# Attention and a mixture of four experts: the first layer of the last three experts as seven block products instead of eight

## The chip, the core and the metric

One core of one Trainium2 chip runs the whole program. Five engines work beside each other: TensorE (PE, matmuls; its weight loads stand as PEld), VectorE (DVE), ScalarE (ACT), GpSimd (POOL) and SyncE (SP), which issues all transfers here. Each runs its own instructions in order and waits for the others by semaphores. The metric is the device time in microseconds (us).

## The reference

```python
def _attn_ref(q, k, v):                       # (2, 8, 576, 64)
    ...
    out_up = np.repeat(out_d, factor, axis=2) # attention over means of 4 rows
    ...
    return (out_up + out_local)               # plus attention within |i - j| < 4

def _moe_ref(x, domain_probs, w1, w2):        # N=1152, D=512, E=4, F=1024
    p = domain_probs / (domain_probs.sum(-1, keepdims=True) + 1e-09)
    for e in range(E):
        h = np.maximum(x @ w1[e], 0.0)
        out += p[:, e:e + 1] * (h @ w2[e])
```

x is the attention's output, 1152 tokens of 512 values. All is float32.

## The kernel before

Steps have names and an engine each. A table, ORDER, puts them in one list, and each engine gets its steps in that order. Attention fills the first 160 us, four half batches a0 to a3, with the matmuls of expert 0 mixed in. Then PE has the experts alone.

An operand of a matmul is split into a high part, rounded to the format that PE takes in one pass, and a low part, the difference. A product is then three: low weight by high x, high by high, high by low. x lies transposed as `xhi` and `xlo`, 4 slices of 128 model values by 1152 tokens. Weights come by 1 MB (`raw`), ACT casts the high part (`whi`, L174), DVE subtracts for the low part (`wlo`, L278), POOL does it for expert 0.

An expert e is done in chunks c of tokens (m00, m01, m02 of 256, m03 of 384; then three of 384 for each of experts 1 to 3). In a chunk, the first layer makes eight tiles of h, f = 0 to 7, each 12 matmuls into one PSUM bank (4 slices of the model by 3 products, `m1`, L734). ACT takes the relu as the high part (`relu`, L741), DVE the low part (`rest`, L745), for the tile of 128 hidden values and all the chunk's tokens. The second layer takes these as weights: 24 matmuls of 512 columns for each 128 tokens (`m2`, L761), and DVE adds the bank, times the token's share, to `acc` (`gather`, L772). The last expert stores its rows. The very last 128 tokens go in two halves of columns.

```python
terms = [(w, x, d) for w, x in ((lo, xhi), (hi, xhi), (hi, xlo)) for d in range(HP)]
for i, (w, x, d) in enumerate(terms):
    nc.tensor.matmul(
        ps[:, :n], w[:, d, cc:cc + P], x[:, d, n0:n0 + n],
```

Buffers of 8 KB a partition are shared, ten in a ring (`s8`): natural rows of q, k and v at first (`k00n`, `v11n`, ...), raw, high and low weights later. PSUM has eight banks: three for the experts (`ps_m`), three for transposes and the like (`ps_g`), two for scores (`ps_s`). SP's loads in the attention are rows of k and q into a part of `acc` (`k11r`, L233), values around a tile of queries (`vw`, L254) and the natural rows (L222).

## Time and profile before

| | |
|---|---|
| runs, us | 495.96, 497.70, 497.76 (median 497.7) |
| span of the profiled execution | 497.3 us, 0.4 below the median |
| PE busy, share of the span | 482.4 us, 97% |
| DVE, ACT, POOL busy | 214.8, 123.5, 54.8 us |
| attention with m00 to m02 | until 160.8 us |
| m03, then experts 1, 2, 3 | from 160.8 us to the end |

The span goes from the first to the last instruction of one profiled execution on the chip. A matmul's record is longer than the distance to the next one, since they are pipelined; what one costs is the length of a run of them divided by their count.

### The profile page before, as it was taken

The page shows a single profiled execution, that of the slowest core. Times are in us where ns is not written, and L with a number is a line of the kernel's source. Part 1 is how long each engine was busy: PE and PEld are TensorE (multiplying, and loading weights), DVE is VectorE, ACT ScalarE, POOL GpSimd, SP SyncE. Part 2 cuts the span into 40 slices and gives each one's busy share as a digit, 9 for nine tenths or more (in the row PEclk, how much of TensorE's full clock was granted, in tenths as well). Part 3 has the DMA queues.
Part 4 walks back from the last instruction along what each step waited for, and adds up shares of the span by engine and source line. Part 5 has one row for each costly group of instructions (what it writes and reads, how often), then busy time and mean ns, then how long its engine had stood idle before and what let it go on. Part 6 is the DMA issues. An engine that isn't in the chain of part 4 may idle for free.

```text
span 497.3 us, 8306 instructions
## 1 busy us (share of the span) xinstructions
PE 482.4 (97%) x3566; PEld 433.8 (87%) x3566; DVE 214.8 (43%) x449; ACT 123.5 (25%) x265; POOL 54.8 (11%) x68
## 2 busy tenths in 40 slices
PE   5999799999999999999999999999999999999997
PEld 5778597888898988989989889899898898998986
DVE  7578858687776252611212516112125261121211
ACT  4555442432231230501101405011014050110110
POOL 4735640140012000000000000000000000000000
PEclk8555989999999999999999999999999999999999
DMA  7893332510600022400000223100002300101001
GB/s 186 206 247 111 77 75 65 123 23 23 213 1 3 0 91 79 153 17 1 0 1 0 77 93 132 38 1 0 1 0 65 105 3 21 43 0 42 22 11 53
DMA packets 39973, 29.88 MB, mean 60 GB/s; under 512 B 26432, under 2 KB 30720, under 8 KB 39936
## 3 DMA queue, kind: packets, MB, share of 16 engines
q1 hardware_dynamic: 39936, 29.35, 20.9%
q8 instruction: 28, 0.46, 0.4%
q14 instruction: 9, 0.07, 0.1%
HBM read 26.99 MB, written 2.36 MB: 59 GB/s over the span
## 4 chain that ended last, share of the span: by engine, by line
PE 91%; DVE 5%; ACT 1%; DMA 1%; issue 1%; SPq 0%; ACTq 0%
PE m03h L734 3%; PE m32h L734 3%; PE m31h L734 3%; PE m30h L734 3%; PE m22h L734 3%; PE m21h L734 3%; PE m20h L734 3%; PE m12h L734 3%; PE m11h L734 3%; PE m10h L734 3%; PE m32o L761 3%; PE m31o L761 3%; PE m30o L761 3%; PE m22o L761 3%; PE m21o L761 3%; PE m20o L761 3%
## 5 line engine op out<-in xcount | busy, mean ns | idle before, releaser
L278 DVE TENSOR_TENSOR wlo<-raw,whi 128x1024 fp32r<-128x1024 f32 x25 | 30.0, 1223 | 5.7 <-ACT whi L174 5.7
L174 ACT CAST whi<-raw 128x1024 fp32r<-128x1024 f32 x32 | 32.3, 1042 | 0.0
L278 POOL TENSOR_TENSOR wlo<-raw,whi 128x1024 fp32r<-128x1024 f32 x7 | 16.7, 2398 | 5.2 <-ACT whi L174 5.1
L761 PE MATMUL m32o<-whi,m32t 128*128 128x512 f32 (+1 forms) x64 | 15.8, 336 | 0.0
L761 PE MATMUL m03o<-whi,m03t 128*128 128x512 f32 x48 | 14.9, 389 | 0.0
L761 PE MATMUL m10o<-whi,m10t 128*128 128x512 f32 x48 | 14.9, 389 | 0.0
L761 PE MATMUL m11o<-whi,m11t 128*128 128x512 f32 x48 | 14.9, 389 | 0.0
L761 PE MATMUL m12o<-whi,m12t 128*128 128x512 f32 x48 | 14.9, 389 | 0.0
L761 PE MATMUL m20o<-whi,m20t 128*128 128x512 f32 x48 | 14.9, 389 | 0.0
L761 PE MATMUL m21o<-whi,m21t 128*128 128x512 f32 x48 | 14.9, 389 | 0.0
L761 PE MATMUL m22o<-whi,m22t 128*128 128x512 f32 x48 | 14.9, 389 | 0.0
L761 PE MATMUL m30o<-whi,m30t 128*128 128x512 f32 x48 | 14.9, 389 | 0.0
L761 PE MATMUL m31o<-whi,m31t 128*128 128x512 f32 x48 | 14.9, 389 | 0.0
L761 PEld LDWEIGHTS m32o<-whi,m32t 128*128 128x128 f32 x64 | 11.1, 190 | 1.2
L761 PE MATMUL m01o<-whi,m01t 128*128 128x512 f32 x32 | 11.5, 412 | 0.0
L761 PE MATMUL m00o<-whi,m00t 128*128 128x512 f32 x32 | 11.2, 407 | 0.0
L741 ACT ACTIVATE m11t<-m11h 128x384 fp32r<-128x384 f32 x8 | 3.9, 492 | 29.3 <-PE m11h L734 29.3
L741 ACT ACTIVATE m12t<-m12h 128x384 fp32r<-128x384 f32 x8 | 3.9, 492 | 29.3 <-PE m12h L734 29.3
L741 ACT ACTIVATE m21t<-m21h 128x384 fp32r<-128x384 f32 x8 | 3.9, 492 | 29.3 <-PE m21h L734 29.3
L741 ACT ACTIVATE m22t<-m22h 128x384 fp32r<-128x384 f32 x8 | 3.9, 492 | 29.3 <-PE m22h L734 29.3
L741 ACT ACTIVATE m31t<-m31h 128x384 fp32r<-128x384 f32 x8 | 3.9, 492 | 29.3 <-PE m31h L734 29.3
L741 ACT ACTIVATE m32t<-m32h 128x384 fp32r<-128x384 f32 x8 | 3.9, 492 | 29.3 <-PE m32h L734 29.3
(388 smaller groups left out, 1217.4 us busy)
## 6 DMA issues: line engine op xcount, KB each, us to landing
raw<-in_moe_w_dram SPq DMA_DIRECT2D x16, 1024.0 KB
vw<-in_v_dram SPq DMA_DIRECT2D x44, 64.0 KB
out_dram<-acc SPq DMA_DIRECT2D x8, 256.0 KB
acc<-in_q_dram SPq DMA_DIRECT2D x12, 144.0 KB
acc<-in_k_dram SPq DMA_DIRECT2D x8, 144.0 KB
q0n<-in_q_dram SPq DMA_DIRECT2D x2, 288.0 KB
k00n<-in_k_dram SPq DMA_DIRECT2D x2, 288.0 KB
k01n<-in_k_dram SPq DMA_DIRECT2D x2, 288.0 KB
```

The lines of the kernel that those rows point to most:

```text
L174: nc.scalar.copy(out_, in_)
L278: engine(f"wlo{nm}.{i}").tensor_tensor(dst, T["raw" + nm][:, sl], T["whi" + nm][:, sl], ALU.subtract)
L734: nc.tensor.matmul(ps[:, :n], w[:, d, cc:cc + P], x[:, d, n0:n0 + n], start=i == 0, stop=i == len(terms) - 1,)
L741: nc.scalar.activation(ht[:, 0, :n], T[f"{nm}h{f}"][:, :n], AF.Relu)
L761: nc.tensor.matmul(ps[:, cs], T[f"{nm}t{f}"][:, hpart, cc:cc + P], w[:, f % 4, cs], start=f == 0 and x == 0, stop=f == KF - 1 and x == 2,)
```

## The change

Experts 1 to 3 get a new first layer. The weights are cut in 2 x 2 (hidden halves by model halves), x as well (model halves by token halves of 576). The eight products of blocks become seven of sums of blocks, with sums shared between them (the form of Strassen's scheme by Winograd). With x's block 11 negated once, most sums of results are additions.

- Sums of x (`sums_of_tokens`): x1, x2, x4 into new tiles `xc`, x3 over block 12, each 576 tokens by 2 slices, in 2 or 3 steps on DVE, split into high and low again by ACT and DVE. Block 11 is negated in place (`xn`). All this stands in ORDER between the matmuls of m03.
- Weights: each expert's first layer in four parts i of 128 + 128 hidden values. A part is loaded into one raw tile r of 7 x 256 (`wl`, 512 KB in two transfers, runs of 512 bytes), three additions on DVE fill places 4 to 6 and rewrite 2 (`ws`), ACT casts the high half (`wh`), DVE makes the low half (`wo`), 1792 elements each. r has one buffer.
- Products (`product`): 12 matmuls of 288 columns, into tiles of two banks, X, Z and Y per part, four such buffers, all of PSUM. Products 1, 6, 7, 4 go one after the other onto X, 5 and 3 onto Z, 2 into Y. Between them results leave X: ACT copies minus X after product 1 and product 6 and minus Z after 5 (`t11`, `t12`, `t22`) and X after 4 (`h21`) into H, and DVE adds Y, Z and X there (`h11`, `h12`, `h22`).
- h stays in float32 (H, all 1152 tokens); relu, high part (`hh`, ACT) and low part (`ho`, DVE) are made per 128 tokens just before the second layer, which runs over nine tiles of tokens and has the matmuls of before (`second`, `g`).
- Second-layer weights come in quarters of 512 KB (`vl`, `vh`, `vo`).
- The ten s8 buffers become five on either side (`s8`, `s8b`); attention's and expert 0's pools end when they are done, and the new tiles take their place. Comments are removed.

A part of the new order, then the core of the code:

```diff
+    p210 t2210 t1210 p710 h1110 vh12 p111 h2210 vo12 p511 t1111 p410 vl11 t2211 p611 h2110 p310 t1211 p211 wo12 p711
...
-    s8 = ctx.enter_context(tc.tile_pool(name="s8", bufs=10))
-    hp_ = ctx.enter_context(tc.tile_pool(name="h", bufs=KF))
-    a1 = ctx.enter_context(tc.tile_pool(name="a1", bufs=1))
-    a2 = ctx.enter_context(tc.tile_pool(name="a2", bufs=2))
-    a3 = ctx.enter_context(tc.tile_pool(name="a3", bufs=3))
-    ps_m = ctx.enter_context(tc.tile_pool(name="ps_m", bufs=3, space=PSUM))
-    ps_s = ctx.enter_context(tc.tile_pool(name="ps_s", bufs=1, space=PSUM))
-    ps_g = ctx.enter_context(tc.tile_pool(name="ps_g", bufs=3, space=PSUM))
+    s8 = ctx.enter_context(tc.tile_pool(name="s8", bufs=5))
+    attn, first, late = ExitStack(), ExitStack(), ctx
+    hp_ = first.enter_context(tc.tile_pool(name="h", bufs=KF, side="right"))
+    s8b = first.enter_context(tc.tile_pool(name="s8b", bufs=5, side="right"))
+    a1 = attn.enter_context(tc.tile_pool(name="a1", bufs=1))
+    a2 = attn.enter_context(tc.tile_pool(name="a2", bufs=2))
+    a3 = attn.enter_context(tc.tile_pool(name="a3", bufs=3))
+    ps_s = first.enter_context(tc.tile_pool(name="ps_s", bufs=1, space=PSUM))
+    ps_g = first.enter_context(tc.tile_pool(name="ps_g", bufs=3, space=PSUM))
+    ps_m = first.enter_context(tc.tile_pool(name="ps_m", bufs=3, space=PSUM))
...
+    def end_attention():
+        attn.close()
+        pool = late.enter_context(tc.tile_pool(name="xc", bufs=1, reuse_waits="tile"))
+        for m in (1, 2, 4):
+            T[f"xc{m}"] = pool.tile([P, 2, 2, NH], F32R, name=f"xc{m}")
+        T["w7"] = late.enter_context(tc.tile_pool(name="w7", bufs=1, reuse_waits="tile"))
+        T["xsums"] = token_sums.enter_context(tc.tile_pool(name="xs", bufs=1, reuse_waits="tile"))
+    def end_sums():
+        token_sums.close()
+        T["qpool"] = late.enter_context(tc.tile_pool(name="q", bufs=2, reuse_waits="tile"))
+    def end_first():
+        first.close()
+        pool = late.enter_context(tc.tile_pool(name="H", bufs=1, side="right", reuse_waits="tile"))
+        T["H"] = pool.tile([P, KF // 2, 2, N], F32, name="H")
+        T["hpool"] = late.enter_context(tc.tile_pool(name="hs", bufs=2, side="right", reuse_waits="tile"))
+        T["w8"] = late.enter_context(tc.tile_pool(name="w8", bufs=2, side="right", reuse_waits="tile"))
+        T["ps"] = late.enter_context(tc.tile_pool(name="ps", bufs=4, space=PSUM, reuse_waits="tile"))
...
+        def add(m, s, x, op, y, deps):
+            def emit():
+                if f"xs{m}" not in T:
+                    T[f"xs{m}"] = T["xsums"].tile([P, 2, NH], F32, tag=f"xs{m}", name=f"xs{m}")
+                at = lambda z: T[f"xs{m}"] if z is None else f32(z)
+                engine(s).tensor_tensor(T[f"xs{m}"], at(x), at(y), op)
+            step(s, "V", deps, emit)
...
+        def split(m, s, deps, out_):
+            step(f"{s}.h", "A", deps, lambda: copy(f"{s}.h", out_()[0], T[f"xs{m}"]))
+            step(f"{s}.l", "V", [f"{s}.h"], lambda: engine(f"{s}.l").tensor_tensor(
+                out_()[1], T[f"xs{m}"], f32(out_()[0]), ALU.subtract))
...
+        own = lambda m: lambda: (T[f"xc{m}"][:, 0], T[f"xc{m}"][:, 1])
+        sub, plus = ALU.subtract, ALU.add
+        read = [f"m03.m{f}" for f in range(KF)]
+        add(1, "x1.s0", B11[1], sub, B12[1], last + ["endattn"])
+        add(1, "x1.s1", None, plus, B11[0], ["x1.s0"])
+        add(1, "x1.s2", None, sub, B12[0], ["x1.s1"])
+        split(1, "x1", ["x1.s2"], own(1))
+        add(1, "x2.s0", None, plus, B22[1], ["x1.l"])
+        add(1, "x2.s1", None, plus, B22[0], ["x2.s0"])
+        split(1, "x2", ["x2.s1"], own(2))
+        add(1, "x4.s0", B21[1], sub, None, ["x2.l"])
+        add(1, "x4.s1", None, plus, B21[0], ["x4.s0"])
+        split(1, "x4", ["x4.s1"], own(4))
+        add(3, "x3.s0", B12[1], sub, B22[1], last + ["endattn"])
+        add(3, "x3.s1", None, plus, B12[0], ["x3.s0"])
+        add(3, "x3.s2", None, sub, B22[0], ["x3.s1"])
+        split(3, "x3", ["x3.s2", "x1.s2"] + read, lambda: B12)
+        for i, s in enumerate(("xn.h", "xn.l")):
+            step(s, "A", ["x1.s2", "m02.m7"] + ([] if i == 0 else []),
+                 lambda i=i: nc.scalar.mul(B11[i], f32(B11[i]), -1.0))
...
+        def load1(i):
+            r = T[f"r{e}{i}"] = T["w7"].tile([P, 7, 256], F32, tag="w7", name=f"r{e}{i}")
+            src = w1[e].rearrange("(c p) (r i f) -> i r p c f", p=P, i=4, f=P)
+            for h in range(2):
+                nc.sync.dma_start(r[:, 2 * h:2 * h + 2].rearrange("p k (d f) -> p (k d) f", d=2), src[i, h])
+        def sums1(i):
+            r, g = T[f"r{e}{i}"], engine(f"ws{e}{i}")
+            g.tensor_tensor(r[:, 4:6], r[:, 0:4:3], r[:, 2:3].to_broadcast([P, 2, 256]), ALU.add)
+            g.tensor_tensor(r[:, 2], r[:, 5], r[:, 0], ALU.add)
+            g.tensor_tensor(r[:, 6], r[:, 1], r[:, 2], ALU.add)
+        def high1(i):
+            w = T[f"wh{e}{i}"] = s8.tile([P, 7, 256], F32R, tag="s8", name=f"wh{e}{i}")
+            copy(f"wh{e}{i}", w, T[f"r{e}{i}"])
+        def low1(i):
+            w = T[f"wo{e}{i}"] = s8.tile([P, 7, 256], F32R, tag="s8", name=f"wo{e}{i}")
+            engine(f"wo{e}{i}").tensor_tensor(w, T[f"r{e}{i}"], f32(T[f"wh{e}{i}"]), ALU.subtract)
+        for i in range(4):
+            step(f"wl{e}{i}", "S", ["endattn"], lambda i=i: load1(i))
+            step(f"ws{e}{i}", "V", [f"wl{e}{i}"], lambda i=i: sums1(i))
+            step(f"wh{e}{i}", "A", [f"ws{e}{i}"], lambda i=i: high1(i))
+            step(f"wo{e}{i}", "V", [f"wh{e}{i}"], lambda i=i: low1(i))
...
+        def high2(q):
+            pool, tag = (s8, "s8") if q < 2 else (T["w8"], "w8")
+            w = T[f"v{e}{q}"] = pool.tile([P, 2, 1024], F32R, tag=tag, bufs=5 if q < 2 else 2, name=f"v{e}{q}")
+            copy(f"vh{e}{q}", w[:, 0], T[f"q{e}{q}"])
+        def low2(q):
+            w = T[f"v{e}{q}"]
+            engine(f"vo{e}{q}").tensor_tensor(w[:, 1], T[f"q{e}{q}"], f32(w[:, 0]), ALU.subtract)
...
+        tokens = {"1": lambda: B11, "5": lambda: (T["xc1"][:, 0], T["xc1"][:, 1]),
+                  "6": lambda: (T["xc2"][:, 0], T["xc2"][:, 1]), "2": lambda: B21, "7": lambda: B12,
+                  "4": lambda: (T["xc4"][:, 0], T["xc4"][:, 1]), "3": lambda: B22}
+        PRODUCTS = {"1": (0, "X", True, "xn.l"), "5": (5, "Z", True, "x1.l"), "6": (2, "X", False, "x2.l"),
+                    "2": (1, "Y", True, "a3.xl2"), "7": (4, "X", False, "x3.l"), "4": (3, "X", False, "x4.l"),
+                    "3": (6, "Z", False, "a3.xl2")}
+        def product(m, i):
+            k, acc_, first_, _ = PRODUCTS[m]
+            if first_:
+                T[f"{acc_}{e}{i}"] = T["ps"].tile([P, 2, 512], F32, tag="ps", name=f"{acc_}{e}{i}")
+            ps = T[f"{acc_}{e}{i}"]
+            hi, lo = tokens[m]()
+            wh, wo = T[f"wh{e}{i}"][:, k], T[f"wo{e}{i}"][:, k]
+            terms = [(w, x, d) for w, x in ((wo, hi), (wh, hi), (wh, lo)) for d in range(2)]
+            for n in range(2):
+                for u, (w, x, d) in enumerate(terms):
+                    nc.tensor.matmul(
+                        ps[:, n, :NH // 2], w[:, d * P:(d + 1) * P], x[:, d, n * (NH // 2):(n + 1) * (NH // 2)],
+                        start=u == 0 and first_, stop=u == 5, skip_group_check=True,
+                    )
+        def into(i, c):
+            at = lambda n: T[f"{n}{e}{i}"][:, :, :NH // 2]
+            dst = H()[:, i, int(c[1]) - 1, (int(c[2]) - 1) * NH:int(c[2]) * NH].rearrange("p (n t) -> p n t", n=2)
+            if c[0] == "t":
+                nc.scalar.mul(dst, at("Z" if c == "t22" else "X"), -1.0)
+            elif c == "h21":
+                nc.scalar.copy(dst, at("X"))
+            else:
+                nc.vector.tensor_tensor(dst, dst, at({"h11": "Y", "h12": "Z", "h22": "X"}[c]), ALU.add)
+        old = [] if e == 1 else [f"ho{e - 1}{t}" for t in range(1, NTOK)] + [f"ho{e - 1}0.{u}" for u in range(2)]
+        wait = {"6": ["t11"], "7": ["t12"], "4": ["h22"], "3": ["t22"]}
+        for i in range(4):
+            for m, (_, _, _, x) in PRODUCTS.items():
+                deps = [f"wo{e}{i}", x, "endfirst"] + [f"{c}{e}{i}" for c in wait.get(m, [])]
+                step(f"p{m}{e}{i}", "P", deps, lambda m=m, i=i: product(m, i))
+            for c, eng, m in (("t11", "A", ["1"]), ("t22", "A", ["5"]), ("t12", "A", ["6"]), ("h22", "V", ["7"]), ("h21", "A", ["4"]),
+                              ("h11", "V", ["2"]), ("h12", "V", ["3"])):
+                more = old if c[0] == "t" or c == "h21" else [f"t{c[1:]}{e}{i}"]
+                step(f"{c}{e}{i}", eng, [f"p{x}{e}{i}" for x in m] + more, lambda i=i, c=c: into(i, c))
...
+        def hrows(t, u):
+            x = H()[:, :, :, t * P:(t + 1) * P]
+            x = x.rearrange("p i r t -> p (i r) t")
+            return x if u is None else x[:, 4 * u:4 * u + 4]
+        def htile(n, t, u):
+            if f"{n}{e}{t}" not in T:
+                T[f"{n}{e}{t}"] = T["hpool"].tile([P, KF, P], F32R, tag=n, name=f"{n}{e}{t}")
+            x = T[f"{n}{e}{t}"]
+            return x if u is None else x[:, 4 * u:4 * u + 4]
+        def hhigh(t, u):
+            nc.scalar.activation(htile("hh", t, u), hrows(t, u), AF.Relu)
+        def hlow(t, u):
+            nc.vector.scalar_tensor_tensor(
+                htile("ho", t, u), hrows(t, u), 0.0, f32(htile("hh", t, u)), ALU.max, ALU.subtract
+            )
+        def final(t):
+            return e == E - 1 and t == NTOK - 1
+        def second(t, v, q):
+            cs = slice(0, DM) if v is None else slice(v * 256, v * 256 + 256)
+            o = f"o{e}{t}{v}"
+            if q == 0:
+                T[o] = T["ps"].tile([P, 512], F32, tag="ps", name=o)
+            for f in (2 * q, 2 * q + 1):
+                for x, (hpart, w) in enumerate((("ho", 0), ("hh", 1), ("hh", 0))):
+                    nc.tensor.matmul(
+                        T[o][:, cs], T[f"{hpart}{e}{t}"][:, f % 4 * 2 + f // 4],
+                        T[f"v{e}{q}"][:, w, f % 2 * 512 + cs.start:f % 2 * 512 + cs.stop],
+                        start=f == 0 and x == 0, stop=f == KF - 1 and x == 2,
+                    )
```

On PE, the first layer of expert 2 begins before like this (m20, first tile of h):

```order
L734 MATMUL m20h0_3107<-xhi_84,wlo120_3032 128x384 [waits DVE_49]
L734 MATMUL m20h0_3107<-xhi_84,wlo120_3032 128x384 x3
L734 MATMUL m20h0_3107<-xhi_84,whi120_3030 128x384 [waits Activation_49]
L734 MATMUL m20h0_3107<-xhi_84,whi120_3030 128x384
L734 MATMUL m20h0_3107<-xhi_84,whi120_3030 128x384 [waits Activation_49]
L734 MATMUL m20h0_3107<-xhi_84,whi120_3030 128x384
L734 MATMUL m20h0_3107<-xlo_85,whi120_3030 128x384 x4
```

and now like this (part 0: products 1, 5 and the begin of 6):

```order
L936 MATMUL X20_3240<-xhi_87,wo20_2974 128x288 x2
L936 MATMUL X20_3240<-xhi_87,wh20_2920 128x288 x2
L936 MATMUL X20_3240<-xlo_88,wh20_2920 128x288 x2
L936 MATMUL X20_3240<-xhi_87,wo20_2974 128x288 x2
L936 MATMUL X20_3240<-xhi_87,wh20_2920 128x288 x2
L936 MATMUL X20_3240<-xlo_88,wh20_2920 128x288 x2
L936 MATMUL Z20_3256<-xc1_2242,wo20_2974 128x288 x2
L936 MATMUL Z20_3256<-xc1_2242,wh20_2920 128x288 x4
L936 MATMUL Z20_3256<-xc1_2242,wo20_2974 128x288 x2
L936 MATMUL Z20_3256<-xc1_2242,wh20_2920 128x288 x4
L936 MATMUL X20_3240<-xc2_2243,wo20_2974 128x288 [waits Activation_49]
```

Twelve matmuls of 384 into one bank have become twelve of 288 into two; Z20 stands between X20 and its next use, which waits for ACT.

On DVE, in the same first layer, before:

```order
L745 SCALAR_TENSOR_TENSOR m20t1_3153<-m20h1_3124,m20t1_3153 128x384 [waits Activation_49]
L278 TENSOR_TENSOR wlo220_3158<-raw220_3120,whi220_3156 128x1024 [waits DMAHW5_49,Activation_49]
L745 SCALAR_TENSOR_TENSOR m20t2_3173<-m20h2_3140,m20t2_3173 128x384 [waits Activation_49]
L278 TENSOR_TENSOR wlo220_3158<-raw220_3120,whi220_3156 128x1024 [waits Activation_49]
L745 SCALAR_TENSOR_TENSOR m20t3_3191<-m20h3_3160,m20t3_3191 128x384 [waits Activation_49]
L278 TENSOR_TENSOR wlo221_3196<-raw221_3122,whi221_3194 128x1024 [waits DMAHW6_49,Activation_49]
```

and now (sums of part 2's weights, h of part 0, the low half wo22):

```order
L878 TENSOR_TENSOR r22_3231<-r22_3231 128x512 [waits DMAHW2_49,DMAHW1_49,DVE_49]
L879 TENSOR_TENSOR r22_3231<-r22_3231 128x256 [waits DVE_49]
L880 TENSOR_TENSOR r22_3231<-r22_3231 128x256 [waits DVE_49]
L949 TENSOR_TENSOR H_2504<-H_2504,Y20_3286 128x576 [waits PE_49,Activation_49]
L949 TENSOR_TENSOR H_2504<-H_2504,X20_3240 128x576 [waits PE_49,Activation_49]
L888 TENSOR_TENSOR wo22_3395<-r22_3231,wh22_3300 128x1792 [waits PE_49,Activation_49]
L949 TENSOR_TENSOR H_2504<-H_2504,Z20_3256 128x576 [waits PE_49]
```

The low half of a weight now stands among additions to H, and it waits for PE, which has still to finish with the buffer it goes to.

On SP, in the attention of the first batch, before (vw05's and vw04's loads, v10n and k11r follow):

```order
L222 DMA v11n_949<-in_v_dram 72x4x256 [waits DMAHW1_49,DVE_49,Pool_49]
L254 DMA vw05_951<-in_v_dram 32x8x64 [waits DMAHW2_49]
L254 DMA vw05_951<-in_v_dram 32x8x64 [waits DMAHW3_49]
L254 DMA vw05_951<-in_v_dram 32x8x64 [waits DMAHW4_49]
L254 DMA vw05_951<-in_v_dram 28x8x64 [waits DMAHW5_49,Pool_49]
```

and now:

```order
L218 DMA v11n_952<-in_v_dram 72x4x256 [waits DMAHW1_49,Activation_49,Pool_49]
L250 DMA vw05_954<-in_v_dram 32x8x64 [waits DMAHW2_49]
L250 DMA vw05_954<-in_v_dram 32x8x64 [waits DMAHW3_49]
L250 DMA vw05_954<-in_v_dram 32x8x64 [waits DMAHW4_49]
L250 DMA vw05_954<-in_v_dram 28x8x64 [waits DMAHW5_49]
```

The load v11n waits for other work of POOL than before; POOL's wlo201, for which v10n waited before, is now what v11n waits for, and v10n no longer waits for it.

## Rows read from the trace of the kernel before

**Rows 1.** the page's busy shares, us, share of the span, instructions
```profile
PE 482.4 (97%) x3566; PEld 433.8 (87%) x3566; DVE 214.8 (43%) x449; ACT 123.5 (25%) x265; POOL 54.8 (11%) x68
```

**Rows 2.** the page's chain that ended last, shares by engine
```profile
PE 91%; DVE 5%; ACT 1%; DMA 1%; issue 1%; SPq 0%; ACTq 0%
```

**Rows 3.** the chain in order of time: start us, us, what
```profile
160.91 16.96 PE m03h L734 x96
177.88 16.32 PE m03o L761 x72
194.19 16.96 PE m10h L734 x96
211.16 16.32 PE m10o L761 x72
...
477.39 16.64 PE m32o L761 x96
```

**Rows 4.** stretches by engine: m03, first layer of expert 1, all of expert 1
```profile
core 0: us, PE busy (x) PEld busy (x) DVE busy (x) ACT busy (x) POOL busy (x), PEclk, DMA share, GB/s
160.75:194.03 33.28, 33.28 (x169) 30.47 (x168) 10.64 (x15) 7.61 (x12) 0.44 (x1) 1.00 0.19 64
194.03:210.99 16.96, 16.96 (x97) 16.95 (x96) 10.05 (x13) 7.18 (x11) 0.00 (x0) 1.00 0.32 103
194.03:293.86 99.83, 99.83 (x505) 91.42 (x504) 30.17 (x42) 19.33 (x32) 0.00 (x0) 1.00 0.14 43
```

**Rows 5.** the same chain, matmuls of 256 columns at the full clock
```profile
102.74 4.25 PE m01h L734 x36
137.41 4.29 PE m02h L734 x36
```

**Rows 6.** groups by line, DVE: busy us, mean ns of one
```profile
L278 DVE TENSOR_TENSOR wlo<-raw,whi 128x1024 fp32r<-128x1024 f32 x25 | 30.0, 1223 | 5.7 <-ACT whi L174 5.7
L745 DVE SCALAR_TENSOR_TENSOR m10t<-m10h,m10t 128x384 fp32r<-128x384 f32 x8 | 4.5, 557 | 5.9 <-ACT m10t L741 5.9
L772 DVE SCALAR_TENSOR_TENSOR acc<-m10o,pr,acc 128x512 f32<-128x512 f32 x3 | 2.3, 751 | 13.7 <-PE m10o L761 13.7
```

**Rows 7.** groups by line, ACT; then a handover in the timeline
```profile
L174 ACT CAST whi<-raw 128x1024 fp32r<-128x1024 f32 x32 | 32.3, 1042 | 0.0
L741 ACT ACTIVATE m10t<-m10h 128x384 fp32r<-128x384 f32 x8 | 3.9, 492 | 21.8 <-PE m10h L734 21.8
...
262.91 0.49 ACT L741 ACTIVATE m12t<-m12h 128x384 fp32r<-128x384 f32 x1 [17.95 <-PE m12h L734]
263.44 0.56 DVE L745 SCALAR_TENSOR_TENSOR m12t<-m12h,m12t 128x384 fp32r<-128x384 f32 x1 [1.89 <-ACT m12t L741]
```

**Rows 8.** stretches of time, the load of 1 MB issued at 181.82 us
```profile
181.80:182.80 1.00, 1.00 (x6) 0.84 (x5) 1.00 (x1) 0.44 (x1) 0.00 (x0) 1.00 0.00 0
182.80:186.80 4.00, 4.00 (x20) 3.30 (x19) 1.26 (x2) 0.00 (x0) 0.00 (x0) 1.00 0.94 305
```

**Rows 9.** timelines of SP, POOL and PE in the attention; chain's longest load
```profile
55.70 0.30 SPq L222 DMA_DIRECT2D v11n<-in_v_dram  x1
56.05 10.72 SPq L254 DMA_DIRECT2D vw<-in_v_dram  x8
67.43 0.94 SPq L233 DMA_DIRECT2D acc<-in_k_dram  x2
...
64.59 2.46 POOL L278 TENSOR_TENSOR wlo<-raw,whi 128x1024 fp32r<-128x1024 f32 x1
...
76.55 0.42 PE L313 MATMUL k11t<-ident,acc 72*128 72x72 f32 x4
...
1.22 4.90 DMA q0n<-in_q_dram
```

**Rows 10.** groups by line, weight loads of PE: busy us, mean ns
```profile
L734 PEld LDWEIGHTS m10h<-xhi,whi 128*128 128x128 f32 x32 | 5.7, 188 | 0.0
L734 PEld LDWEIGHTS m02h<-xhi,whi 128*128 128x128 f32 x32 | 4.3, 188 | 0.0
```

More of the change, by code (lines that the diff above doesn't have):

```diff
@@ L262, in load @@
         def load():
-            t = T["raw" + nm] = s8.tile([P, 4, 512], F32, tag="s8", name="raw" + nm)
+            t = T["raw" + nm] = (s8, s8b)[which - 1].tile([P, 4, 512], F32, tag="s8", name="raw" + nm)
             if which == 1:
@@ new lines, in sums_of_tokens @@
+    def sums_of_tokens():
+        last = [f"a3.xl{t}" for t in range(NT)]
+        step("endattn", "X", last + ["m02.m7"], end_attention)
+        step("endsums", "X", ["x4.l", "x3.l"], end_sums)
+        step("endfirst", "X", ["m03.g2", "endattn"], end_first)
+        def add(m, s, x, op, y, deps):
[29 more added lines that the diff above has]
+                 lambda i=i: nc.scalar.mul(B11[i], f32(B11[i]), -1.0))
@@ L819 @@
             attention(b, half)
-    for e in range(E):
-        for which in (1, 2):
-            for half in range(2):
-                weight(e, which, half)
-        chunks = ((0, 256), (256, 256), (512, 256), (768, 384)) if e == 0 else ((0, 384), (384, 384), (768, 384))
-        for c, (n0, n) in enumerate(chunks):
-            expert(e, c, n0, n)
+    for which in (1, 2):
+        for half in range(2):
+            weight(0, which, half)
+    for c, (n0, n) in enumerate(((0, 256), (256, 256), (512, 256), (768, 384))):
+        expert(0, c, n0, n)
+    sums_of_tokens()
+    for e in range(1, E):
+        late_expert(e)
     plan(steps)
```

245 lines of the change are left out of this document (129 added, 116 removed).

## The prediction

> **What bounds the kernel now.** I read the busy shares first: TensorE (PE) is busy for 482.4 of 497.3 us [rows 1]. A busy PE need not be on the path, so the chain of waits comes next: PE holds 91% of it [rows 2]. Then the chain in order of time: from 160.9 us on it is PE alone, 96 matmuls of a first layer in 16.96 us, 72 of a second in 16.32, in turn, to the last 16.64 us [rows 3]. The stretches by engine agree: one late expert takes 99.83 us, all of it PE at granted clock 1.00, the higher level (2.4 GHz), with VectorE (DVE) at 30.2 and ScalarE (ACT) at 19.3 us beside it [rows 4]. So a late expert costs its matmuls, 3 x 16.96 + 3 x 16.32 = 99.84 us, and what shortens them counts in full as long as the work beside them keeps up.
>
> **First layer: fewer columns, more matmuls.** Before, an expert has 288 matmuls of 384 columns: 50.88 us, 176.7 ns each [rows 3]. After, it has 4 blocks x 7 products x 12 = 336 of 288 columns. No row has 288. At the full clock 36 matmuls of 256 columns took 4.29 us, 119.2 each (another 36: 118.1) [rows 5]; 512 columns take 16.32 / 72 = 226.7 [rows 3]. A straight line from 256 to 384 gives 119.2 + 32/128 x 57.5 = 133.6 ns. Low end: 384 scaled by columns, 132.5. High end: the line through 512 and 384 carried down, 176.7 - 96 x 0.39 = 139.2. I take 133.6, since 256 is the nearest row. 336 x 133.6 = 44.9 us, 6.0 less per expert, **18.0 us less** for three; the ends give 19.1 and 12.3.
>
> **Second layer.** Still 9 x 24 matmuls of 512 columns an expert, the very last tile in halves as before: no change on PE. Beside each tile of 5.44 us ACT has one pass of 1024 elements (1.04), DVE a difference of 1024 (1.22) and the sum into acc (0.75) [rows 6, 7]: hidden.
>
> **What must hide beside a block.** A block is 84 x 133.6 = 11.2 us of PE. From 384 to 1024 elements DVE rows rise by 1.04 ns an element, ACT rows by 0.86 [rows 6, 7]. DVE per block: weight sums of 512, 256 and 256, 1.5; the low half of 1792, 2.0; three additions of 576 out of PSUM at 0.76 to 0.82 (the higher from the row of 751 ns for 512), 2.5; one low half of second-layer weights, 1.2. Sum 7.2 of 11.2. ACT: the high half of 1792, 1.7; four copies of 576 at 0.66; one cast, 1.0: 5.4 of 11.2. The totals fit; three places are narrow.
>
> (a) PE may not add to X again before ACT has copied it. The product on another buffer between them is 12 x 133.6 = 1.6 us, against 0.66 for the copy and 0.04 for a handover (ACT from 262.91 for 0.49, DVE from 263.44 [rows 7]). Hidden, unless ACT is in the middle of a 1.7 us high half.
>
> (b) The low half of block i goes into a buffer that block i-2 read as weights, and the last product of i-2 stands fifth of seven within block i-1. Two products, 3.2 us, are left for a step of 2.0, two handovers and, if DVE is in one, an addition of 0.8: 0.3 us spare.
>
> (c) One raw buffer: a load waits for the low half before it. 1 MB came in 1.0 us of silence and 4.0 at 305 GB/s [rows 8], so half of that needs 3.0 us in runs of the same length; runs of 512 B are not in the trace, and I bound them by 5.0. Load, sums, high, low: 3.0 + 1.5 + 1.7 + 2.0 = 8.2, at most 10.2, of 11.2.
>
> Together these cost 0 at the low end; at the high end each of 12 blocks meets half a DVE addition, 12 x 0.4 = 4.8. I take **1.0 us**, nearer to 0 since each sum fits. If the cover goes, each us of lateness per block costs 12.
>
> **Token sums under the last chunk of expert 0.** On DVE 14 steps of 1152 elements (1.36 each, 19.0), two weight sums and two low halves (7.1) come in, four low halves (4.6) go. DVE was busy 10.6 of 33.3 us there [rows 4]; now some 32. That is nearly full, but the last sum and the last acc of the chunk are first needed four products (6.4 us) into expert 1. Cost 0 to 3, taken 0.5.
>
> **Attention.** One wait moves. SP's queue is in order; the load v11n was issued at 55.70 and now waits for POOL's last low half, which starts at 64.59 and takes 2.46, so until 67.1 [rows 9]. Behind it stand eight vw, v10n and two k11r loads. Before, the first of the last two was issued at 67.43; now 11 issues stand ahead or between at about 0.45 each (two take 0.94), so the second leaves near 72.0 and lands, by the longest load of the chain, 4.90 us [rows 9], at 76.9. PE uses it at 76.55: 0 to 0.4 us late, taken 0. Otherwise the order before m03 is the same but for two swapped low halves on POOL.
>
> **Sum.** 497.3 - 18.0 + 1.0 + 0.5 = 480.8 us of span. The median of the runs, 497.7, lies 0.4 above the profiled span: **481.2 us**. Own range: 497.7 - 19.1 = 478.6 to 497.7 - 12.3 = 485.4, plus up to 4.8 + 3 of waits.
>
> **Rivals.** *A, the weight chain is late:* if 512-byte runs move at half the rate (5.0 us) and two of the steps of (c) find their engine in another step (0.8 on DVE, 0.7 on ACT), the chain is 10.2 + 1.5 + four handovers = 11.9, 0.7 late in the 9 blocks whose load isn't hidden under a second layer: +6.3, 487.5. For it: (c) has least room at its long end; against: 305 GB/s with nothing else on the queues [rows 8].
>
> *B, DVE and ACT run in turn instead of side by side:* both queues are in order, every low half waits for a high half and every addition for a copy. Wholly in turn a block takes 7.2 + 5.4 + a dozen handovers of 0.04 = 13.1 us, 1.9 late, 12 x 1.9 = 23: 504, slower. It decides against the change from 11.2 + 18/12 = 12.7 us a block. Against it: the second layer between experts lets both engines catch up, and most steps do not depend on each other.
>
> *C, a matmul's cost doesn't fall with its columns:* in the first layer the weight loads fill their row, 16.95 of 16.96 us [rows 4], and 336 loads stand where 288 were. At 176.7 ns each that is 59.4 us an expert, 8.5 more, +25.5: 523. It decides from 50.88 / 336 = 151.4 ns a matmul. Against it: loads read 188 ns [rows 10] for 256 columns as well, and those pairs came every 119 ns [rows 5], so loads overlap.
> The Trainium skill, Perfetto Trace Analysis, Identifying the Most-Contended Engine, says to judge TensorE's headroom by the busy share of LDWEIGHTS instead of matmul; by that the first layer has none, and this change adds loads. The same skill, TensorE: Matmul & The Clock Gate, Back-to-back issue gap, gives 81 ns at 128 columns and 131 at 512 for streams of load and matmul; an estimate on its line is 114 at 384 and 102 at 288, hence 336 x 102 - 288 x 114 = +1.4 us an expert, 502. Here 512 columns take 226.7 ns [rows 3], so the trace does not bear that line out.
>
> *D, the products are not fewer than I count:* the order has the 84 matmuls of 288 a block, so only the attention's 0.4 us is left of it.
>
> **Chances.** Forecast (477.5 to 485) 0.75; A and milder forms of it (485 to 492) 0.17; B 0.04, half of it slower than before; C 0.02; anything else 0.02, slower. The range takes in the forecast and the lower half of A: 477.5 to 488.5. About 0.5% (2.5 us) is what a measurement can tell from no change. Faster 0.93, same 0.02, slower 0.05.
>
> **What would show it.** Right: 288-column matmuls every 133 to 139 ns, first layers of 45 to 47 us, PE idle under 3 us after 195 us, its chain still PE alone. (a) wrong: PE waiting for ACT on X; (b) or (c): PE waiting for DVE at a block's first product, at the second to fourth block of an expert; token sums: one wait at the start of expert 1. A shows DVE waiting for loads. C shows in the spacing alone. The forecast fails if the spacing is over 140 ns or PE waits over 0.6 us a block.

## The result, and the profile of the changed kernel

The changed kernel takes 482.0 us (median; 481.7 to 482.5) against 497.5 us before (the median of four runs; the three that were known ahead of the prediction gave 497.7): the ratio is 0.9689, with a 95% interval of 0.9648 to 0.9730. The forecast was 481.2 us with a range of 477.5 to 488.5.

The page of the changed kernel, its busy shares and the chain that ended last by engine, answers to [rows 1] and [rows 2]. It also says how much work came to the other engines: VectorE (DVE) went from 214.8 to 277.8 us, ScalarE (ACT) from 123.5 to 162.7.

```profile
PE 466.3 (97%) x3710; PEld 414.9 (86%) x3710; DVE 277.8 (58%) x493; ACT 162.7 (34%) x277; POOL 54.7 (11%) x68
...
PE 89%; DVE 5%; DMA 3%; SPq 1%; issue 1%; ACT 1%; ACTq 0%
```

TensorE (PE) is busy for the same 97% of a shorter span. The stretches by engine, as [rows 4]: the last chunk of expert 0, the first layer of expert 1, its second layer.

```profile
core 0: us, PE busy (x) PEld busy (x) DVE busy (x) ACT busy (x) POOL busy (x), PEclk, DMA share, GB/s
160.31:193.33 33.02, 33.02 (x170) 30.16 (x170) 31.34 (x34) 13.77 (x16) 0.26 (x1) 1.00 0.11 33
193.33:238.02 44.69, 44.69 (x337) 44.69 (x337) 22.55 (x29) 20.44 (x26) 0.00 (x0) 1.00 0.29 88
238.02:287.82 49.80, 49.80 (x219) 40.55 (x218) 23.50 (x24) 10.76 (x10) 0.00 (x0) 1.00 0.07 21
```

The chain in order of time, as [rows 3]:

```profile
160.31 16.65 PE m03h L730 x96
176.96 16.37 PE m03o L755 x72
193.33 1.60 PE X L936 x12
194.93 1.59 PE Z L936 x12
...
238.02 5.52 PE o10None L993 x24
243.54 5.53 PE o11None L993 x24
...
471.25 5.70 PE o L993 x48
```

From 160.3 us on the chain is PE alone, and no row of waits of PE is left after 195 us. In the first layer a product of 12 matmuls takes 1.596 us, 133.0 ns each; in the second layer a tile of 24 takes 5.53 us, where a third of the 16.32 us in [rows 3] is 5.44. The difference of the two spans, 497.3 - 480.2 = 17.1 us, is made of

| stretch | before, us | after, us | difference |
|---|---|---|---|
| up to the last chunk of expert 0 | 160.91 | 160.31 | -0.6 |
| last chunk of expert 0 | 33.28 | 33.02 | -0.3 |
| first layers of experts 1 to 3 | 3 x 50.88 | 3 x 44.69 | -18.6 |
| second layers of experts 1 to 3 | 3 x 48.96 + 0.3 | 2 x 49.80 + 49.95 | +2.3 |

(The last 128 tokens, in two halves, make the 0.3 before and the 0.15 after.) The first layers gave what was forecast, no wait took anything away, and the second layers, which the change leaves with the same matmuls (624 of 512 columns, 48 of 256), became 2.3 us longer. That loss, and the room that the three narrow places really have, are what the experiments are about.

### The profile page after: what moved, and what is told of

It is laid out like the page before. It is cut to its first block, busy times and chain, and to the rows that moved or that the text cites. A ratio compares the mean times of both kernels' runs of the same rounds, so it can differ in the third digit from the quotient of the medians.

```text
span 480.2 us, 8723 instructions
## 1 busy us (share of the span) xinstructions
PE 466.3 (97%) x3710; PEld 414.9 (86%) x3710; DVE 277.8 (58%) x493; ACT 162.7 (34%) x277; POOL 54.7 (11%) x68
## 4 chain that ended last, share of the span: by engine, by line
PE 89%; DVE 5%; DMA 3%; SPq 1%; issue 1%; ACT 1%; ACTq 0%
PE X L936 16%; PE Z L936 8%; PE Y L936 4%; PE m03h L730 3%; PE m03o L755 3%; DMA k01n<-in_k_dram 2%; PE m02h L730 2%; PE m01o L755 2%; PE m01h L730 2%; PE m02o L755 2%; PE m00o L755 2%; PE m00h L730 2%; DVE ptb L556 1%; PE o L993 1%; PE o28None L993 1%; PE o18None L993 1%
## 5 line engine op out<-in xcount | busy, mean ns | idle before, releaser
L975 ACT ACTIVATE hh<-H 128x1024 fp32r<-128x1024 f32 (+1 forms) x30 | 28.9, 974 | 92.1 <-PE o10None L993 4.9
L978 DVE SCALAR_TENSOR_TENSOR ho<-H,hh 128x1024 fp32r<-128x1024 f32 (+1 forms) x30 | 33.6, 1119 | 24.5 <-ACT hh L975 24.5
L888 DVE TENSOR_TENSOR wo<-r,wh 128x1792 fp32r<-128x1792 f32 x12 | 24.3, 2023 | 22.8 <-PE Z L936 18.9
L936 PE MATMUL X<-xc,wh 128*128 128x288 f32 x192 | 33.2, 295 | 0.0
L936 PEld LDWEIGHTS X<-xc,wh 128*128 128x128 f32 x192 | 28.2, 188 | 0.0
L936 PE MATMUL X<-xhi,wo 128*128 128x288 f32 x96 | 20.7, 296 | 0.0
L936 PE MATMUL X<-xlo,wh 128*128 128x288 f32 x96 | 20.6, 296 | 0.0
L936 PE MATMUL X<-xhi,wh 128*128 128x288 f32 x96 | 20.6, 295 | 0.0
L936 PE MATMUL X<-xc,wo 128*128 128x288 f32 x96 | 20.5, 295 | 0.0
L170 ACT CAST wh<-r 128x1792 fp32r<-128x1792 f32 x12 | 20.3, 1689 | 0.3 <-DVE r L880 0.3
```

The costliest lines, as they stand in the source:

```text
L170: nc.scalar.copy(out_, in_)
L888: engine(f"wo{e}{i}").tensor_tensor(w, T[f"r{e}{i}"], f32(T[f"wh{e}{i}"]), ALU.subtract)
L936: nc.tensor.matmul(ps[:, n, :NH // 2], w[:, d * P:(d + 1) * P], x[:, d, n * (NH // 2):(n + 1) * (NH // 2)], start=u == 0 and first_, stop= ...
L975: nc.scalar.activation(htile("hh", t, u), hrows(t, u), AF.Relu)
L978: nc.vector.scalar_tensor_tensor(htile("ho", t, u), hrows(t, u), 0.0, f32(htile("hh", t, u)), ALU.max, ALU.subtract)
```

## Where the second layer lost 2.3 us

A second-layer matmul holds a 128 x 128 piece of an h tile as its weights and streams 512 columns of the second-layer weight matrix past it (the moving operand). The row of one tile of tokens, from the view of one tile's instructions (min, median and max of a record's ns), of the changed kernel and then of the first experiment:

```profile
L993 PE MATMUL o11None<-v,hh x16: 387/392/398, 243.6 to 248.7; 128*128 128x512 f32 x16
```

```profile
L994 PE MATMUL o11None<-v,hh x16: 389/389/389, 244.4 to 249.3; 128*128 128x512 f32 x16
```

In the kernel before, as in the experiment, each record lasts 389 ns and matmuls come every 226.7; in the changed kernel records last 387 to 398 ns and matmuls come every 230.5 on average, in the same pattern in every tile, down to a nanosecond or two. Work on other engines would not repeat like that. The granted clock is 1.00 in both stretches. Something fixed was the suspect, and the program's memory map shows one: in the kernel before, the h tiles and all weights begin at the same remainder modulo 512 bytes (96). In the changed kernel the h tiles and two of the four quarters of second-layer weights lie on the right-hand side of SBUF, at 480, and the other two quarters on the left, at 96.

**Putting the remainders alike.** The edit is one line, an unused tile:

```diff
+    ctx.enter_context(tc.tile_pool(name="padr", bufs=1, side="right")).tile([P, 96], F32, name="padr")
     hp_ = first.enter_context(tc.tile_pool(name="h", bufs=KF, side="right"))
```

> The changed kernel with one unused 384-byte tile at the bottom of the right-hand side of SBUF, so that the h tiles (hh, ho) and all four quarters of second-layer weights begin at the same remainder modulo 512 bytes (96); in the changed kernel the h tiles and quarters 2 and 3 begin at 480, quarters 0 and 1 at 96. Same instructions, same order. Theory P (placement: a 512-column matmul runs slower when its moving operand and the weights loaded beside it start at different remainders): second-layer matmuls of experts 1 to 3 return from 230.5 to 226.7 ns, each second layer from 49.8 to 49.0 us, the whole 2.5 us faster than the changed kernel, 479.5 us. Rival W (work beside: it is the steps of ScalarE and VectorE per tile or the waits at a tile's first matmuls that slow it): spacing stays at 230.5, 482 us.

Measured: 479.7 us, ratio to the kernel before 0.9656 (0.9632 to 0.9680). The stretches of its last chunk of expert 0 and of the second layer of expert 1:

```profile
160.88:194.15 33.27, 33.27 (x170) 30.46 (x170) 31.35 (x34) 13.91 (x16) 0.28 (x1) 1.00 0.11 33
238.84:287.82 48.98, 48.98 (x218) 40.55 (x218) 23.50 (x24) 10.79 (x10) 0.00 (x0) 1.00 0.07 23
```

The second layer is back at 48.98 us, 226.7 ns a matmul, beside the same 23.5 us of DVE. Theory P holds, W falls.

**The opposite edit on the kernel before.** An unused tile of 128 bytes ahead of the h tiles:

```diff
+    ctx.enter_context(tc.tile_pool(name="pad", bufs=1)).tile([P, 32], F32, name="pad")
     hp_ = ctx.enter_context(tc.tile_pool(name="h", bufs=KF))
```

> The kernel before with one unused 128-byte tile between the ring of raw and weight buffers and the tiles of h: weights stay at remainder 96 modulo 512 bytes, h tiles go to 224. Nothing else differs. Theory P: its 512-column matmuls in the late experts go from 226.7 to about 230.5 ns, 72 x 3.8 = 0.27 us a chunk, nine chunks 2.5 us, about 500 us. Rival W: 226.7 ns stay, 497.5 us.

Measured: 499.7 us. The chain in order of time, a first and a second layer of expert 1:

```profile
193.63 16.65 PE m10h L735 x96
210.28 16.79 PE m10o L762 x72
```

The second layer of a chunk went from 16.32 to 16.79 us, 233.2 ns a matmul: more than the 230.5 expected, since here every moving operand is unlike its weights, where in the changed kernel half of them are. At the same time the first layer fell from 16.96 to 16.65, which nobody had forecast.

One trace of the changed kernel says the same by itself. A tile takes the quarters in the order left, right, left, right, six matmuls each. By the starts of the records, the matmuls on a left quarter, which are unlike, come 237 and 229 ns apart in turn after the first two (234 and 225); in the experiment all 72 of a second layer do. On a right quarter, which is alike, they come 230 to 232 ns apart at first and 226 to 228 from the fourth on. An unused tile shifts everything that lies behind it, so the two experiments alone could blame another tile; this spacing changes with the quarter, inside one kernel.

**How wide the period is.** The same edit with 256 bytes ([P, 64]):

> The kernel before with an unused tile of 256 bytes (not 128) between the ring of weight buffers and the tiles of h: weights at remainder 96 modulo 512 bytes, h tiles at 352. Theory P with a period of 512 bytes: still unlike, 512-column matmuls at 230 to 233 ns, as with 128 bytes. Theory P with a period of 256 bytes or less: alike again, 226.7 ns.

```profile
191.07 16.96 PE m10h L735 x96
208.03 16.32 PE m10o L762 x72
```

16.32 again, and 16.96 for the first layer. (The span, 494.2 us, is 3.1 below that of before because the last chunk of expert 0 began 3.1 us earlier, at 157.6 us; more on that below.) So of periods of 512, 256 and 128 bytes only 256 fits: 128 bytes apart is unlike, 256 alike. Other distances were not tried with 512 columns.

**All tiles alike.** In all kernels above the tiles of tokens begin at 128, the weights that are held against them in the first layer at 96. Here all of these tiles begin at 128:

```diff
+    ctx.enter_context(tc.tile_pool(name="padr", bufs=1, side="right")).tile([P, 88], F32, name="padr")
     hp_ = first.enter_context(tc.tile_pool(name="h", bufs=KF, side="right"))
...
-    wz = big.tile([P, 64], F32, name="wz")
+    wz = big.tile([P, 72], F32, name="wz")[:, :64]
```

> The changed kernel with unused tiles of 32 bytes on the left and 352 on the right side of SBUF: weights, h tiles and token sums all begin at remainder 128 modulo 512 bytes, as the tokens do (in the other kernels weights begin at 96, 32 bytes off the tokens). Theory P: second layers at 226.7 ns. On the 384-column matmuls of the last chunk of expert 0, seen at 176.7 (the kernel before, first run) and at 173.4 (the changed kernel, the kernel before with 128 bytes shifted): if the 32 bytes between tokens and weights are what costs 3.3 ns there, 173.4; if it is what the matmuls before them left behind, 176.7 as in the first run. 288 columns at 133.0 in either case, the whole 479.5 us.

The chain, the last chunk of expert 0, a product, a tile of the second layer:

```profile
160.12 16.66 PE m03h L731 x96
176.78 16.36 PE m03o L756 x72
193.15 1.58 PE X L937 x12
...
243.20 5.44 PE o11None L994 x24
```

384 columns at 173.5 ns (16.66 / 96), 512 at 226.7, and a product at 1.58 to 1.59 us instead of 1.59 to 1.60. With 288 columns the placement makes little: the second half of a product's columns starts 1152 bytes behind the first, so 128 bytes off modulo 256, here as in the changed kernel, and in that one the token sums' first halves (alike) came every 132.1 ns, their second halves (unlike) every 132.7. A single execution took 479.2 us. Timed in rounds against the kernel before:

> The same kernel as in the run with all remainders alike, timed in rounds against the kernel before. Theory P: 2.5 us below the changed kernel by the second layers and 0.3 to 1 by the first (288 columns came at 132.7 to 132.8 ns instead of 133.0), 479.0 us; the start of the last chunk of expert 0 lay between 157.6 and 161.8 us in the traces so far, for either kernel, so single times may differ by 2 us. Rival: the gain is no more than that spread, 482 us.

Measured: 480.0 us (479.2 to 482.4), ratio 0.9656 (0.9629 to 0.9683). By the time alone the rival stands; the spans at the end of this section settle it.

**The unused tile only under the late experts,** to keep 173.4 ns in the last chunk of expert 0:

```diff
+        pool = late.enter_context(tc.tile_pool(name="padr", bufs=1, side="right", reuse_waits="tile"))
+        pool.tile([P, 96], F32, name="padr")
         pool = late.enter_context(tc.tile_pool(name="H", bufs=1, side="right", reuse_waits="tile"))
```

> The changed kernel with the unused 384-byte tile only under the late experts' tiles (h in float32, hh, ho, quarters 2 and 3 of the second-layer weights), so that the last chunk of expert 0 keeps the placement of the changed kernel. Theory P: second layers at 226.7 ns a matmul, 2.5 us less than the changed kernel; the 384-column matmuls of the last chunk of expert 0 stay at 173.4 ns, 0.3 us better than with the tile at the bottom of the side (176.7 there): 479.4 us. Rival: the 384-column spacing is not a matter of that stage's placement and is 176.7 again: 479.7 us.

Measured: 479.5 us, ratio 0.9649 (0.9608 to 0.9689), with 173.4 ns for 384 columns and 226.7 for 512. The three versions with like remainders are 2.0 to 2.5 us below the changed kernel by their medians, but the intervals of their ratios overlap with its own (0.9648 to 0.9730), so the times alone do not show the gain.

The traces do. From the first record of the last chunk of expert 0 to the end, which leaves out how early the attention happened to be done, the changed kernel takes 320.1 us; the version with like second layers 318.0, that with the tile under the late experts 317.8, and that with all tiles alike 317.5 in both of its traces. Each is 2.1 to 2.6 us shorter, as the spacings say.

## How much room the three narrow places have

With no wait in the profile, the prediction's places (a), (b) and (c) could not be read off; each was given more work until it gave way. The times below are of single executions; what counts is where PE waits in the trace, and the span from the start of the last chunk of expert 0 (320.1 us in the changed kernel by its records).

**(b), the low half twice.** In the changed kernel the low half of block i, released by product 3 of block i-2, and the addition behind it on DVE:

```profile
303.35 2.03 DVE L888 TENSOR_TENSOR wo<-r,wh 128x1792 fp32r<-128x1792 f32 x1 [6.69 <-PE Z L936]
305.29 0.75 DVE L949 TENSOR_TENSOR H<-H,Z 128x576 f32<-128x576 f32 x1
```

and PE's first product of the next block, on the PSUM tile that this addition sets free:

```profile
306.81 0.43 PE L936 MATMUL X<-xhi,wo 128*128 128x288 f32 x2
```

The edit:

```diff
-            engine(f"wo{e}{i}").tensor_tensor(w, T[f"r{e}{i}"], f32(T[f"wh{e}{i}"]), ALU.subtract)
+            for _ in range(2):
+                engine(f"wo{e}{i}").tensor_tensor(w, T[f"r{e}{i}"], f32(T[f"wh{e}{i}"]), ALU.subtract)
```

> The changed kernel with every low half of the first-layer weights of experts 1 to 3 computed twice, the same result into the same buffer: 2.0 us more of VectorE in the step that stands between the release of a buffer by product 3 and the first product that needs it. By the prediction's place (b), 0.3 us spare: PE waits 1.7 us in each of about 10 blocks, +17 us, 499 us. By the trace of the changed kernel (buffer free at 303.3, low half done at 305.4, first use at 306.8: 1.4 us spare, because the release comes with the last matmul that reads the low half and no addition stands in the way): PE waits 0.6 us in the third and fourth block of each expert, +3.6 us, 486 us. If VectorE had room everywhere: no change, 482 us.

Measured: 494.7 us, 10.7 more from the start of the last chunk of expert 0. Waits of PE after 190 us (us in total, times, longest), then DVE and PE at one of them:

```profile
PE X L937 <- DVE H L950: 7.6, 6, 1.4
PE X L937 <- ACT H L946: 0.8, 1, 0.8
```

```profile
211.89 4.08 DVE L889 TENSOR_TENSOR wo<-r,wh 128x1792 fp32r<-128x1792 f32 x2 [5.48 <-PE Z L937]
215.90 0.75 DVE L950 TENSOR_TENSOR H<-H,Z 128x576 f32<-128x576 f32 x1
```

```profile
216.70 0.53 PE L937 MATMUL X<-xhi,wo 128*128 128x288 f32 x2 [1.11 <-DVE H L950]
```

PE idles for 0.8 to 1.4 us at a time, not for the 0.6 that the low half alone explains, nor for the 1.7 of the prediction. (The rows hold 8.4 of the 10.7 us: a record outlasts the distance to the next one, and the matmuls behind a wait come late as well, 0.53 us for a pair instead of 0.43; the last chunk of expert 0 is 0.4 us longer.) What the product waits for, in six of the seven cases, is the addition H<-H,Z: PSUM is a ring of four tiles, and the next block's X takes the tile that the addition reads, which stands behind the low half on DVE's queue. It ends at 305.29 + 0.75 = 306.04 in the changed kernel and PE comes at 306.81: 0.8 us to spare, and 2.0 - 0.8 is the mean of 1.2 seen (8.4 / 7). My expectation had counted the low half's own reader (1.4 us) and missed the one behind it. And only seven products wait: the third and fourth block of each expert and the second of expert 1. The first two blocks of experts 2 and 3 have their weights made ready under the second layer before them, so a step's lateness does not count twelve times.

**(c), the load twice,** the second issued after the first has landed:

```diff
             for h in range(2):
-                nc.sync.dma_start(r[:, 2 * h:2 * h + 2].rearrange("p k (d f) -> p (k d) f", d=2), src[i, h])
+                for _ in range(2):
+                    nc.sync.dma_start(r[:, 2 * h:2 * h + 2].rearrange("p k (d f) -> p (k d) f", d=2), src[i, h])
```

> The changed kernel with each load of raw first-layer weights of experts 1 to 3 issued twice, the same bytes into the same buffer, the second after the first has landed: it lengthens the chain load, sums, high, low by one load or two (3.4 us for both halves in the changed kernel's trace). Rival A of the prediction (the chain has about 1 us of room a block): PE late by over 2 us in each of nine blocks, +18 us or more, 500 us. Theory of a slack chain (by the trace of the changed kernel 9.0 us from issue to the low half's end, of a period of 11.17, and the wait that ends last before a low half is that for product 3): late only where loads follow each other block on block, third and fourth block, 0 to 2 us each, 482 to 490 us.

Measured: 501.4 us. That is what rival A was to give, yet not for its reason. The load of the changed kernel, issued at 305.40 and used by DVE from 308.95:

```profile
305.40 12.29 SPq L874 DMA_DIRECT2D r<-in_moe_w_dram  x4
```

```profile
308.95 0.69 DVE L878 TENSOR_TENSOR r<-r 128x512 f32<-128x512 f32 x1 [1.11 <-DMA r<-in_moe_w_dram]
```

so 3.55 us for 512 KB in runs of 512 bytes, between the prediction's ends of 3.0 and 5.0. In the experiment SP's issues begin at 317.14 and the sums at 327.22, 10.1 us later: the four pieces come one after the other, 6.5 us more than in the changed kernel, the upper end of the one or two loads (3.4 to 6.8) that I had expected.

```profile
317.14 15.86 SPq L875 DMA_DIRECT2D r<-in_moe_w_dram  x5
```

```profile
327.22 0.69 DVE L879 TENSOR_TENSOR r<-r 128x512 f32<-128x512 f32 x1 [7.65 <-DMA r<-in_moe_w_dram]
```

```profile
331.15 0.53 PE L937 MATMUL X<-xhi,wo 128*128 128x288 f32 x2 [2.87 <-ACT H L946]
```

```profile
PE X L937 <- ACT H L946: 12.1, 4, 6.0
PE X L937 <- DVE H L950: 1.4, 3, 0.8
```

(the last two rows: all waits of PE after 190 us.) Of the 6.5 us PE sees 2.9 in this block, so the chain had 3.6 us to spare. The waiting product is not the one that needs the new weights: it adds to X, and waits for ACT's copy, because ACT's queue is in order and the high half, itself waiting for the late sums, stands ahead of the copy. Place (c) gives way through place (a). The longest wait, 6.0 us, is in the second block of expert 1, whose chain starts inside the crowded last chunk of expert 0; it is the largest part of what my 482 to 490 us lacked.

**The same 2.0 us of DVE elsewhere.** Is it DVE's total that ran out, or the place? The first weight sum four times:

```diff
-            g.tensor_tensor(r[:, 4:6], r[:, 0:4:3], r[:, 2:3].to_broadcast([P, 2, 256]), ALU.add)
+            for _ in range(4):
+                g.tensor_tensor(r[:, 4:6], r[:, 0:4:3], r[:, 2:3].to_broadcast([P, 2, 256]), ALU.add)
```

> The changed kernel with the first of the three weight sums of each block done four times (the same operands, the same result): 3 x 0.68 = 2.0 us more of VectorE a block, as much as the doubled low half added, but ahead of the high half instead of between the freed buffer and the next block. Theory place: only where a step stands in the program costs; the chain load, sums, high, low has 3.4 us to spare (the doubled loads made it 15.5 us and the last block 3.0 us late), so 2.0 us more fit: 482 to 483 us. Theory total: VectorE's work per block is what ran out with the doubled low half, so the same 2.0 us cost the same 10 us: 492 us.

Measured: 485.1 us. One wait of PE is left after 192 us, and the last chunk of expert 0 is longer:

```profile
159.64:193.67 34.03, 33.61 (x171) 30.12 (x170) 33.61 (x39) 13.43 (x16) 0.26 (x1) 1.00 0.08 25
```

```profile
PE X L937 <- ACT H L946: 2.5, 1, 2.5
```

In that chunk DVE, busy for 31.34 of 33.02 us in the changed kernel, is now busy for 33.61, the chunk is 1.0 us longer, and PE idles for 0.4 us of it. DVE comes out of it so late that the sums for the second block of expert 1 end 4 us later than in the changed kernel, and ACT's queue shows the same jam: high half, two copies, then PE at 202.5.

```profile
199.68 1.69 ACT L170 CAST wh<-r 128x1792 fp32r<-128x1792 f32 x1 [3.66 <-DVE r L881]
201.27 0.65 ACT L946 ACTIVATE H<-Z 128x576 f32<-128x576 f32 x1
201.81 0.64 ACT L946 ACTIVATE H<-X 128x576 f32<-128x576 f32 x1
```

In the other ten blocks the same 2.0 us cost nothing. So place holds, total falls, with one exception that bears out the prediction's remark on the token sums: there DVE's total is what counts, and about 1.5 us (4 us later, 2.5 us waited) are left.

**(a), the copies twice,** by a function of the same two lines called ahead of them:

```diff
+            if c[0] == "t" or c == "h21":
+                for _ in range(1):
+                    copy_out(c, dst, at)
             if c[0] == "t":
                 nc.scalar.mul(dst, at("Z" if c == "t22" else "X"), -1.0)
```

> The changed kernel with ScalarE's four copies out of PSUM in each block done twice (the same result): 0.65 us more between a product and the next one on the same buffer, 2.6 us of ScalarE a block. Place (a) of the prediction gives 1.6 us for a copy: two of 0.65 and 0.2 for the handovers are 1.5 and fit, and PE waits only where a copy stands behind a high half of 1.7 us or a cast of 1.0: 482 to 486 us. If copies had no cover: 36 copies out of X by 0.65, +23 us, 505 us.

Measured: 485.3 us, 2.8 more from the start of the last chunk of expert 0. Two copies of X by ACT, then PE:

```profile
199.52 0.64 ACT L943 ACTIVATE H<-X 128x576 f32<-128x576 f32 x1
200.20 0.65 ACT L954 ACTIVATE H<-X 128x576 f32<-128x576 f32 x1
```

```profile
200.90 0.54 PE L936 MATMUL X<-xhi,wo 128*128 128x288 f32 x2 [0.57 <-ACT H L954]
```

The copy pair began late, behind a high half and a doubled copy of Z, and PE waited 0.6 us; once in each expert a product on X came 0.25 us late; elsewhere two copies all but fit between two products on X, whose matmuls come every 135.3 ns for 133.0. Where ACT comes to the copy free, place (a) has 0.7 us of room, not the 0.9 that the sum of the prediction left (1.6 - 0.7): in the changed kernel the first copy of expert 1 ends 0.68 us before the next matmul on X.

```profile
195.03 0.65 ACT L945 ACTIVATE H<-X 128x576 f32<-128x576 f32 x1 [4.62 <-PE X L936]
```

```profile
196.36 0.43 PE L936 MATMUL X<-xc,wo 128*128 128x288 f32 x2
```

The copy doubled, that matmul starts 0.06 us late.

## What a matmul of fewer columns costs

Rival C held that weight loads set the spacing. The products were cut into three pieces of 192 columns:

```diff
-            for n in range(2):
+            for n in range(3):
...
-                        ps[:, n, :NH // 2], w[:, d * P:(d + 1) * P], x[:, d, n * (NH // 2):(n + 1) * (NH // 2)],
+                        flat[:, 320 * n:320 * n + 192], w[:, d * P:(d + 1) * P], x[:, d, n * 192:(n + 1) * 192],
```

> The changed kernel with each product's 576 tokens in three pieces of 192 columns instead of two of 288: 126 matmuls a block instead of 84, the same columns. By the spacings measured so far (256: 119.2, 288: 133.0, 384: 173.4, 512: 226.7 ns; that is columns at 2.4 GHz plus 12.5 to 13.4 ns): 192 at 80 + 13 = 93 ns, a block 11.75 instead of 11.17 us, 12 blocks +7 us, 489 us. Rival C of the prediction (weight loads set the spacing): 192 columns come no faster than the 119 ns of 256, a block 15.0 us, +46 us, 528 us.

Two of the three pieces share a PSUM bank and each begins its sum there, which changes the sums that go into h; the matmuls, their columns and the work beside them are as described, and the time is read for these. Measured: 517.0 us. Two products in the chain, and the first layer of expert 1 by engine:

```profile
193.50 1.99 PE X L937 x18
195.49 2.01 PE Z L937 x18
```

```profile
193.49:250.10 56.61, 56.61 (x508) 56.52 (x507) 23.50 (x30) 21.13 (x26) 0.00 (x0) 1.00 0.25 75
```

A product of 18 takes 2.01 us, 111.6 ns a matmul, and PE waits for nothing. That is neither the 93 ns of columns alone nor the 119 of rival C. A floor would explain it, with C's mechanism: below some column count between 192 and 256 a pair of weight load and matmul would come no faster than about 112 ns. That is argued and not shown, since one width below 256 was run; 128 columns at 112 ns as well would show it. From 256 on the columns set the time: 256 at 119.2, 288 at 133.0, 384 at 173.4 (in the changed kernel), 512 at 226.7, each its columns at 2.4 GHz plus 12.5 to 13.4 ns. With 288 columns this change stays 21 ns above those 112. On the Trainium skill's rule that the prediction named (Perfetto Trace Analysis, Identifying the Most-Contended Engine): LDWEIGHTS fills its row in the first layer before and after (16.95 of 16.96 us, 44.69 of 44.69) and the layer still got shorter by 12%, so here that share alone does not say what headroom there is.

## Why the prediction was right, step by step

- **The bound.** PE alone held the path, and what shortened its matmuls counted in full: -18.6 us in the first layers, -18.0 forecast. 133.6 ns were taken, 133.0 measured; the straight line from 256 towards 384 was the right choice of the three, and the 0.6 ns between them, over 1008 matmuls, are the 0.6 us.
- **Second layer: "no change on PE".** This is the step that failed: +2.3 us. It counted instructions and their columns, which are the same, and took for granted that a matmul of 512 columns costs 226.7 ns wherever its operands lie. The runs with unused tiles, and the spacing by quarters in the changed kernel itself, showed that their placement relative to each other decides between 226.7 and up to 233.2.
- **Waits in the blocks,** +1.0 taken: 0. The low end was right, each sum fitted. The spares measured are 0.7 us for (a), where 0.9 was reckoned, 0.8 for (b), where 0.3 was reckoned, and 3.6 for (c), where 1.0 to 3.0 was reckoned. For (b) the size was near and the waiter was wrong: not the low half's reader but the addition queued behind it.
- **"Each us of lateness per block costs 12":** too many. The doubled low half was late in seven blocks, the doubled load in fewer.
- **Token sums,** +0.5 taken: 0 (the chunk even took 0.3 us less, its 384-column matmuls coming at 173.4 instead of 176.7 ns). DVE was busy for 31.3 us, 32 forecast, and the room behind it is about 1.5 us.
- **Attention,** 0 taken: -0.6. SP's load v11n left at 66.7 (67.1 forecast) and k11t began no later. The start of the last chunk of expert 0 lay between 157.6 and 161.8 us over thirteen traces of both kernels and their variants, so 0.6 is nothing that these runs can tell from chance.
- **From span to time,** +0.4 taken: the time is 1.7 to 1.9 us above the span in all executions here but one (2.1), in the changed kernel 1.8 (482.0 and 480.2). The profiled execution of before, 497.3, thus stood for some 499.1, 1.4 above the median of 497.7 that the prediction used. The span was forecast at 480.8 and came 0.6 below, at 480.2; this term was 1.4 too small, and the two make the 0.8 between 481.2 and 482.0.
- **Rivals.** A and B did not happen: no DVE wait for a load cost PE anything. C fell at 288 columns, 133.0 ns against its 176.7; at 192 the spacing is above what the columns cost, by a cause that is not shown. D did not happen: a first layer has the 336 matmuls that were counted.

That the forecast was within 0.8 us is partly luck: a loss of 2.3 that it lacked met 1.5 of waits that it had and did not need, 0.6 each from the columns and the attention and 0.3 from the last chunk of expert 0, and the some 0.6 that these left over met the 1.4 from span to time. Its mechanism, PE alone on the path with fewer columns in all, was right; the second layer, the waits and the step from span to time were mis-sized.

## What to carry to other kernels

Fewer columns in all pay even in more matmuls, as long as each matmul stays in the range where its columns set its time (here seen from 256 to 512); read where that ends from a run with small pieces, not from the busy share of the loads. When a change moves tiles to another side or pool, compare the spacing of the matmuls that it did not touch, and if it moved, compare where the two operands start. A place in an in-order queue is narrow for what stands behind the step that you look at: ask what the next two instructions on that engine set free.
